# Transposing the queries, keys and attention outputs of three of four batches by DMA in place of TensorE

## The chip, the cores and the metric

The kernel runs on one core of one Trainium2 chip. The metric is the device time of one execution in microseconds (us). Before the change it is 679.26 us, the median of two runs (679.05 to 679.47).

## What is computed

A sparse attention over q, k and v (4 batches, 8 heads, 768 positions, 64 dims) is followed by a mixture of experts over its 3072 output rows. Cut to what matters:

```python
k_sum = k.reshape(B, H, nb, 32, D).max(axis=3)        # 24 blocks of 32 keys
v_sum = v.reshape(B, H, nb, 32, D).mean(axis=3)
scores_l = scale * q @ k^T, only where |i - j| < 16
scores_s = scale * q @ k_sum^T + log(32)
a = softmax(concat(scores_l, scores_s)); attn = a @ concat(v, v_sum)
x = attn with heads side by side                      # (3072, 512)
P = exp(x @ w_gate - max), 8 rounds of row and column normalization
out = sum over e of P[:, e] * (relu(x @ w1[e]) @ w2[e])   # 8 experts, 512 -> 1024 -> 512
```

## The kernel before, in words

Two heads make a pair: NP = 16 pairs, PB = 4 for each batch, numbered 0 to 15. S = 768 positions are G = 6 groups of 128. For each pair TensorE needs keys and queries with the head dimension on the partitions (kT and qT, 128 x 768, the two heads above one another), but they arrive with positions on the partitions. POOL loads them with a cast to bf16 (`load_qk`, L255; `load_v`, L271) into rings of NQ = 6 buffers.

Pairs 0 to 3 (batch 0) go in halves (`pair_half`, L654), so that expert 0 can begin early. Pairs 4 to 15 go whole (`pair_start`, L622, and `pair_whole`, L683). For a whole pair:

- `tr` (L295): six TensorE transposes of 128x128 into a PSUM bank, once for the keys (z = 0) and once for the queries (z = 1). `tr_out` (L307) copies the 128x768 result to kT or qT on ACT, or, for queries, on ACT or DVE.
- `key_max` (L315) on DVE reduces kT to the 24 block maxima. `block_sums` and `block_out` (L327, L334) make the block sums of v.
- `near_values` (L346): four DMAs from SP that copy rows of v next to a group's borders into V_e.
- `scores`, `score_exp`, `masks`, `edges`, `summaries2`, `summary_exp` and `values` (L356 to L431) make the local and summary scores, their exponentials and the weighted values. `normalize` (L487) divides, on DVE, into xs (positions on the partitions).
- `to_xT` (L502): six TensorE transposes of xs into a PSUM bank. `x_out` (L509) copies the result to xT, the input of the experts, on ACT or DVE.

PSUM banks of the attention are a ring "a" of NA = 3. A whole pair opens eight of them: two for `tr`, one for the block sums, two for the summaries, two for the values, one for `to_xT`.

Buffers that set waits: kT and qT have NB = 4 buffers, so that the transposes of pair i wait for the scores, key maxima and summaries of pair i - 4; a load of keys or queries waits for the `tr` of pair i - 6; v's load waits for the values of pair i - 6; V_e and E_e have two.

The order of the work up to the end of the attention comes from a planner (class `Plan`, L34). Each piece of work is a unit with an engine, a booked cost in us, the units that it depends on, a priority (a lower number goes first) and, where it ends later than its engine is free, a `lag`. The planner repeatedly takes the unit that can start first on its engine, and among those within 0.02 us the one of lowest priority number. The instructions are issued in that order, and each engine executes its own in order. Attention pairs have priorities 20 + i, expert 0's matmuls 1000 and more, so that expert 0 fills TensorE between the attention's pieces. Expert 0 works on half a batch (384 rows) at a time: 8 hidden groups of 4 matmuls (L200) and 6 of 4 for the projection (L210); the halves of a batch start when all four pairs of that batch are in xT. Copies out of PSUM get a priority 100 lower. `near_values` is booked with 0.4 us on SP and a lag of 3.5.

`late_constants` (L591) zeroes E_e and V_e, which pairs from 4 on use, sets the ones of V_e and a constant of the routing. It is one unit of 2.4 us on DVE.

After the attention the row and column normalization (`bridge`, L1054) runs beside the rest of expert 0 and the first groups of expert 1, and experts 1 to 7 follow in an order written out by hand (from L1144 on): the lines L877 and L883 of the profile.

Of the kernel before, what the change touches and what calls it, by code (L numbers as in the profile page):

```python
# [33 lines left out]
class Plan:  # L34
# [12 lines left out]
    def add(self, eng, cost, fn, deps=(), prio=0.0, opens=(), uses=(), lag=0.0):  # L47
        u = Unit(eng, cost, fn, [d for d in deps if d is not None], prio, list(opens), lag)
        for b in list(opens) + list(uses):
            b.users.append(u)  # L50
        if uses and eng != "PE":
            u.prio -= 100.0
        self.waiting.append(u)
        return u
# [62 lines left out]
def kernel(  # L117
# [10 lines left out]
    nc = tc.nc  # L128

    B, H, S, D = q.shape  # L130
    G = S // 128
    N, DM = out.shape
    E = moe_w_gate.shape[1]
# [5 lines left out]
    PB = H // 2  # L139
    SCALE = 1.0 / float(D) ** 0.5  # L140
    W = 16
# [4 lines left out]
    VD = D + 1  # L146
# [9 lines left out]
    col_en = const.tile([128, 128], FP32)  # L156
# [3 lines left out]
    xT = persist.tile([128, KD, N], FP16)  # L160
# [34 lines left out]
    def copy(eng, out, in_):  # L195
        (nc.scalar.copy if eng == "ACT" else nc.vector.tensor_copy)(out=out, in_=in_)
# [18 lines left out]
    NB = PB  # L215
    NE = 2
# [9 lines left out]
    if True:  # L226
# [4 lines left out]
        qT = [attn.tile([128, W + S + W], BF16, name=f"qT{i}") for i in range(NB)]  # L231
        kT = [attn.tile([128, S], BF16, name=f"kT{i}") for i in range(NB)]
# [6 lines left out]
        E_e = [attn.tile([128, G, 128], BF16, name=f"Ee{i}") for i in range(NE)]  # L239
        V_e = [attn.tile([128, G, 2 * VD], BF16, name=f"Ve{i}") for i in range(NE)]  # L240

        plan = Plan({"m": 3, "s": NS, "a": NA})
        add = plan.add

        at, units = {}, {}
# [49 lines left out]
        def tr(i, z, tag):  # L295
            st = at.pop(("st", i, z))
            t = at["t", i, z] = bank(tag, "tkq", BF16)
            for g in range(G):
# [4 lines left out]
                else:  # L303
                    nc.tensor.transpose(t[:, g * 128:(g + 1) * 128],  # L304
                                        st[:, g, :, :].rearrange("p j d -> p (j d)"), ident)

        def tr_out(eng, i, z):  # L307
            r, src = i % NB, at.pop(("t", i, z))[:, 0:S]
            dst = (kT[r][:], qT[r][:, W:W + S])[z]
            if i < PB:  # L310
                dst = dst.rearrange("c (p g) -> c p g", g=G)
                src = src.rearrange("c (g p) -> c p g", g=G)
            copy(eng, dst, src)
# [32 lines left out]
        def near_values(i):  # L346

            sv, ve = v_x[i % NQ], V_e[i % NE]
            for j in range(2):
                c0, q0 = VD * j, 64 + 32 * j  # L350
                nc.sync.dma_start(out=ve[q0 + W:q0 + 2 * W, 1:G, c0:c0 + VD],
                                  in_=sv[128 - W:128, j, 0:G - 1, :])
                nc.sync.dma_start(out=ve[q0:q0 + W, 0:G - 1, c0:c0 + VD],
                                  in_=sv[0:W, j, 1:G, :])

        def scores(i, h):  # L356
# [145 lines left out]
        def to_xT(i, h=None):  # L502
            t = at.pop(("xs", i, h or 0))
            tx = at["tx", i, h] = bank("a", "tx", FP16)
            for g in range(G if h is None else HG):
                nc.tensor.transpose(tx[:, g * 128:(g + 1) * 128],  # L506
                                    t[:, g, :, :].rearrange("p j d -> p (j d)"), ident16)

        def x_out(eng, i, h=None):  # L509
            n, t0 = (S, 0) if h is None else (HS, h * HS)  # L510
            t0 += i // PB * S
            copy(eng, xT[:, i % PB, t0:t0 + n], at.pop(("tx", i, h))[:, 0:n])
# [76 lines left out]
            nc.vector.tensor_copy(out=wg_bf[:], in_=wg_f32[:])  # L589

        def late_constants():  # L591
            for t in E_e:
                nc.vector.memset(t[64:128, :, :], 0.0)
            for t in V_e:
                nc.vector.memset(t[:], 0.0)
                nc.vector.memset(t[0:24, :, D:VD], 32.0 / XS)
                nc.vector.memset(t[32:56, :, VD + D:2 * VD], 32.0 / XS)
            nc.vector.memset(col_en, float(E) / float(N))


        U = {}
# [20 lines left out]
        def pair_start(i, prio):  # L622
            o = i - NB
            war_k = [U.get(("S", o, 0)), U.get(("S", o, 1)), U.get(("km", o))]
            war_q = war_k[:2] + [U.get(("ss", o, 0)), U.get(("ss", o, 1))]
            tag = "m" if i < PB else "a"
            for z in range(2 if i >= PB else 1):
                buf = Buffer(tag)
                U["tr", i, z] = add("PE", 0.4, lambda z=z: tr(i, z, tag),
                                    [U["kq"[z], i], U["ident"]] + (war_k, war_q)[z]  # L630
                                    + [U["tr", i, 0] if z else U.get(("S", i - 1, 1 if i > PB else 0))],
                                    prio, opens=[buf])
                U["kT", i, z] = add({"ACT": 0.8} if z == 0 else {"ACT": 0.8, "DVE": 0.95},
                                    0, lambda z=z: tr_out(U["kT", i, z].on, i, z), [U["tr", i, z]], prio,
                                    uses=[buf])
            if i < PB:
                query_half(i, 0, prio)
            U["km", i] = add("DVE", 0.95, lambda: key_max(i), [U["kT", i, 0]] + war_q[2:], prio)
            buf = Buffer("a")
            U["vs", i] = add("PE", 0.4, lambda: block_sums(i),  # L640
                             [U["v", i]] + ([U.get(("A", i - NE, 1))] if i >= PB else []), prio + 0.01, opens=[buf])
            U["Vs", i] = add("DVE", 0.36 if i < PB else 0.84, lambda: block_out(i), [U["vs", i]],
                             prio + 0.01, uses=[buf])
# [37 lines left out]
            return U.get((what, n % PB, n // PB)) if n >= 0 else None  # L681

        def pair_whole(i, prio):  # L683
            U["near", i] = add("SP", 0.4, lambda: near_values(i), [U["v", i], U.get(("A", i - NE, 1))], prio,
                               lag=3.5)
            for h in range(2):
                buf = Buffer("s")
                U["S", i, h] = add("PE", 0.28, lambda h=h: scores(i, h),
                                   [U["kT", i, 0], U["kT", i, 1], U.get(("ed", i - 2))], prio, opens=[buf])
                U["X", i, h] = add("ACT", 0.97, lambda h=h: score_exp(i, h), [U["S", i, h]], prio, uses=[buf])  # L690
                U["mk", i, h] = add("DVE", 0.56, lambda h=h: masks(i, h),
                                    [U["X", i, h], U.get(("A", i - 2, 1))], prio)
            U["ed", i] = add("DVE", 0.78, lambda: edges(i),
                             [U["X", i, 0], U["X", i, 1], U["mk", i, 1], U.get(("A", i - NE, 1))], prio)
            bufs = [Buffer("a"), Buffer("a")]
            U["ss", i, 0] = U["ss", i, 1] = add("PE", 0.22, lambda: summaries2(i),
                                                [U["km", i], U["kT", i, 1], U.get(("A", i - NE, 1))], prio,
                                                opens=bufs)
            for h in range(2):
                U["sx", i, h] = add("ACT", 0.46, lambda h=h: summary_exp(i, h), [U["ss", i, h]], prio,  # L700
                                    uses=[bufs[h]])
            for h in range(2):
                buf = Buffer("a")
                U["A", i, h] = add("PE", 0.4, lambda h=h: values(i, h),
                                   [U["mk", i, h], U["ed", i], U["sx", i, h], U["Vs", i], U["near", i]],
                                   prio, opens=[buf])
                U["no", i, h] = add("DVE", 0.68, lambda h=h: normalize(i, h),
                                    [U["A", i, h], U.get(("xt", i - 2))], prio, uses=[buf])
            buf = Buffer("a")
            U["xt", i] = add("PE", 0.35, lambda: to_xT(i), [U["no", i, 0], U["no", i, 1]], prio, opens=[buf])  # L710
            U["x", i] = add({"ACT": 0.8, "DVE": 0.9}, 0, lambda: x_out(U["x", i].on, i), [U["xt", i]], prio,
                            uses=[buf])

        halves, zero = [], []

# [52 lines left out]
        c0 = add("DVE", 3.8, constants, [], -5.0)  # L768
        for i in range(PB):
            pair_start(i, i)  # L770
            pair_half(i, 0, i)
        add("DVE", 2.4, late_constants, [U["mk", PB - 1, 0]], 5.5)
        expert0(0, [U["x", i, 0] for i in range(PB)])
        for i in range(PB):
            pair_half(i, 1, 10 + i)
# [2 lines left out]
        for i in range(PB, NP):  # L778
# [3 lines left out]
            if i % PB == PB - 1:  # L782
                b = i // PB
                xs = [U["x", PB * b + d] for d in range(PB)]
# [24 lines left out]
    if True:  # L809
# [340 lines left out]
        g = q = NOTHING  # L1150
        for n in range(LAG, len(groups)):
            g0, q0 = g, q
            g = group(*groups[n])
            q = pair(*groups[n - LAG])
            e, j, i = groups[n]
# [55 lines left out]
        A, B, C, D = last  # L1211
# [42 lines left out]
```

The softmax here doesn't subtract the row's maximum and nothing guards it: scores larger than these inputs give would overflow.

## Time and profile before

| what | value |
|---|---|
| median of the runs | 679.26 us |
| the profiled execution | 684.06 us, its span 681.4 us |
| granted clock of TensorE, mean | 0.992 |
| TensorE transposes of pairs 4 to 15: keys, queries (L304) | 72 + 72, 219 to 220 ns each |
| TensorE transposes of outputs (L506), pairs 4 to 15 among 96 | 72 of 128x128 |
| copies to kT, qT, xT of pairs 4 to 15 (L196) | 36 of 128x768: on ACT 0.80 us each, on DVE 0.55 to 0.56 |
| first transposition of pair 4, last of pair 15 | 37.9 us, 127.6 us |
| loads of keys, queries, values on POOL | 0.86, 0.86 and 1.04 us to issue; 6.0, 5.8 and 6.5 us to landing |
| near values on SP | 48 DMAs of 10.2 KB, 0.6 us to issue, 4.6 us to landing |

All are of one profiled execution except the median. PE is TensorE, PEld its loads of weights (they overlap PE), DVE VectorE, ACT ScalarE, POOL GpSimd, SP the engine that here only issues DMAs; an engine's name with a q (SPq, POOLq) is its queue of DMA issues. L304 is line 304 of the kernel. A group row of the profile has line, engine, operation, output <- input with shapes and count, then busy time and the mean ns of one, then the idle time of the engine just before it with what ended it. A timeline row has start, duration, engine, line and what was done. "To landing" is from the issue of a DMA to the arrival of its data.

### The profile page before, as it was taken

To read this page: it belongs to the slowest core of one execution; us is meant where nothing else is said; L and a number is where in the kernel's file an instruction comes from. 1 tells how busy PE (TensorE), PEld (TensorE's weight loads), DVE (VectorE), ACT (ScalarE), POOL (GpSimd) and SP (SyncE) were. 2 spreads that over 40 slices of the span, in tenths; PEclk is the share of its full clock that TensorE was granted. 3 is DMA by queue.
4 is the path that set the end of the run, shared out by engine and by line. 5 is a ranking of instruction groups with operands and counts; after the bars stand their busy time and mean duration, and the time that the engine had idled before them with its cause. 6 is when DMAs were issued, how large, how long until landed. Compare 5 with 4: busy or idle time off the path is not lost.

```text
span 681.4 us, 13654 instructions
## 1 busy us (share of the span) xinstructions
PE 670.5 (98%) x5189; PEld 441.6 (65%) x5189; DVE 585.4 (86%) x1445; ACT 407.7 (60%) x788; POOL 125.9 (18%) x165
## 2 busy tenths in 40 slices
PE   8999999999999999999999999999999999999996
PEld 4665666545666666666666666666666666666665
DVE  6778898788599988999889988998899888998886
ACT  4677877656677765555555555555555555555551
POOL 8699630022202010100101010201010101100000
PEclk9799999999999999999999999999999999999999
DMA  9999990000503123310513050404131051301224
GB/s 120 188 143 143 98 144 7 1 1 0 78 1 37 12 31 48 31 17 1 78 17 33 1 78 1 48 1 60 19 31 17 7 72 17 32 1 48 78 93 155
DMA packets 113618, 33.90 MB, mean 50 GB/s; under 512 B 99984, under 2 KB 110736, under 8 KB 113552
## 3 DMA queue, kind: packets, MB, share of 16 engines
q0 software_dynamic: 104672, 26.22, 41.6%
q1 hardware_dynamic: 8352, 6.80, 3.3%
q8 instruction: 40, 0.66, 0.4%
q14 instruction: 26, 0.21, 0.1%
q10 hardware_dynamic: 528, 0.02, 0.0%
HBM read 52.45 MB, written 6.29 MB: 86 GB/s over the span
## 4 chain that ended last, share of the span: by engine, by line
PE 92%; DVE 4%; DMA 1%; issue 1%; ACT 1%; POOL 1%; DVEq 0%; ACTq 0%
PE xy L883 36%; PE pg L877 16%; PE pa L877 10%; PE pb L877 10%; PE yps L210 6%; PE hps L200 6%; PE sg L323 1%; PE tkq L304 1%; PE vs L331 1%; PE av L468 1%; PE tx L506 1%; DMA qst<-in_q_dram 1%; DVE out_acc L1018 1%; PE av L395 1%; PE av L401 1%
## 5 line engine op out<-in xcount | busy, mean ns | idle before, releaser
L883 PEld LDWEIGHTS <-hf 128*128 128x128 f16 x2352 | 230.1, 98 | 96.1 <-issue 1.2
L883 PE MATMUL xy<-w,hf 128*128 128x256 f16 x1312 | 183.4, 273 | 0.1
L883 PE MATMUL xy<-ws,hf 128*128 128x256 f16 x984 | 147.6, 273 | 0.1
L191 ACT ACTIVATE hf<-pg 128x512 f16<-128x512 f32 x84 | 50.2, 597 | 149.6 <-PE pg L877 149.4
L1018 DVE SCALAR_TENSOR_TENSOR out_acc<-xy,P_sb,out_acc 128x512 f32<-128x512 f32 x164 | 115.1, 744 | 1.7 <-PE xy L883 1.7
L824 DVE TENSOR_TENSOR hf<-hf 128x512 f16<-128x512 f16 x252 | 99.6, 422 | 8.8
L877 PE MATMUL pa<-xT,w 128*128 128x512 f16 x336 | 99.9, 379 | 0.0
L877 PEld LDWEIGHTS <-w 128*128 128x128 f16 x672 | 65.8, 98 | 43.6 <-issue 0.6
L827 DVE TENSOR_TENSOR hf<-pb,c 128x512 f16<-128x512 f32 x84 | 58.1, 692 | 38.2 <-PE pb L877 35.7
L176 POOL DMA_DIRECT2D w<-in_moe_w_dram x56 | 41.8, 759 | 220.3 <-PE pg L877 192.1
L877 PEld LDWEIGHTS <-ws 128*128 128x128 f16 x504 | 49.3, 98 | 25.3
L911 ACT COPY c<-pg 128x512 f32<-128x512 f32 x84 | 49.2, 585 | 22.7 <-PE pg L877 22.6
L827 DVE TENSOR_TENSOR hf<-pg,c 128x512 f16<-128x512 f32 x84 | 57.2, 681 | 0.6 <-PE pg L877 0.6
L191 ACT ACTIVATE hf<-pa 128x512 f16<-128x512 f32 x84 | 50.6, 603 | 0.4 <-PE pa L877 0.4
L896 ACT COPY pg<-pa 128x512 f32<-128x512 f32 x84 | 47.9, 570 | 4.8
L877 PE MATMUL pg<-xTs,w 128*128 128x512 f16 x168 | 50.0, 379 | 0.1
L877 PE MATMUL pb<-xT,ws 128*128 128x512 f16 x168 | 50.0, 379 | 0.0
L877 PE MATMUL pg<-xTs,ws 128*128 128x512 f16 x168 | 50.0, 379 | 0.0
L877 PE MATMUL pg<-xT,w 128*128 128x512 f16 x168 | 50.0, 379 | 0.0
L877 PE MATMUL pb<-xTs,ws 128*128 128x512 f16 x168 | 50.0, 379 | 0.0
L904 ACT COPY c<-pb 128x512 f32<-128x512 f32 x84 | 49.8, 593 | 0.2 <-ACT pg L896 0.2
L200 PE MATMUL hps<-xT,w 128*128 128x384 f16 x256 | 48.7, 326 | 0.0
(136 smaller groups left out, 842.5 us busy)
## 6 DMA issues: line engine op xcount, KB each, us to landing
w<-in_moe_w_dram POOLq DMA_DIRECT2D x8, 1024.0 KB, 9.3
w<-in_moe_w_dram POOLq DMA_DIRECT2D x56, 128.0 KB, 3.5
out_dram<-out_acc SPq DMA_DIRECT2D x22, 256.0 KB, 2.0
qst<-in_q_dram POOLq DMA_DIRECT2D x32, 96.0 KB, 5.8
vx<-in_v_dram POOLq DMA_DIRECT2D x16, 192.0 KB, 6.5
kst<-in_k_dram POOLq DMA_DIRECT2D x24, 96.0 KB, 6.0
w<-in_moe_w_dram POOLq DMA_DIRECT2D x2, 512.0 KB, 8.3
kst<-in_k_dram POOLq DMA_DIRECT2D x4, 192.0 KB, 4.9
```

Source lines behind the costliest of these rows:

```text
L176: nc.gpsimd.dma_start(out=t[:, :, h, :], in_=moe_w1[e].rearrange("(dk p) f -> p dk f", p=128)[:, :, f:f + 128])
L191: nc.scalar.activation(out=out, in_=in_, func=AF.Relu, bias=0.0, scale=1.0)
L200: nc.tensor.matmul(hp[:, 0:n], lhsT=w1s[e][:, dk, 128 * f:128 * (f + 1)], rhs=xT[:, dk, t0:t0 + n], start=(dk == 0), stop=(dk == KD - 1))
L210: nc.tensor.matmul(yp[:], lhsT=h[:, f, c * 128:(c + 1) * 128], rhs=w2s[e][:, f, :], start=(f == 0), stop=(f == KF - 1))
L824: nc.vector.tensor_tensor(out=out, in0=in0, in1=in1, op=ALU.subtract)
L827: nc.vector.tensor_tensor(out=out, in0=in0, in1=in1, op=ALU.add)
L877: nc.tensor.matmul(bank[:], lhsT=w[:, dk, :], rhs=x[:, dk, :], start=start and dk == 0, stop=dk == KH - 1, skip_group_check=True)
L883: nc.tensor.matmul(bank, lhsT=a(f)[:, 128 * c:128 * (c + 1)], rhs=w[:, f, :], start=start and f == 0, stop=f == FH - 1, skip_group_check=True)
L896: nc.scalar.copy(out=B["g"][:], in_=B["a"][:])
L904: nc.scalar.copy(out=B["c5"][:], in_=B["b"][:])
L911: nc.scalar.copy(out=B["c2"][:], in_=B["g"][:])
L1018: nc.vector.scalar_tensor_tensor(out=acc, in0=src, scalar=P_sb[:, t, e:e + 1], in1=acc, op0=ALU.mult, op1=ALU.add)
```

## The change

For pairs 4 to 15 the keys, queries and outputs are transposed by one DMA each from SBUF to SBUF, issued from SP (`tr_dma`, `x_dma`), where they were six TensorE transposes and a copy out of PSUM. Each is booked with 0.1 us on SP and a lag of 2.6. No bank of ring "a" is opened for them. The other dependencies stay, except that a pair's transposes no longer wait for the scores of the pair before or for each other. `late_constants` returns a list of pieces, which are chained on DVE with priority 12.5 in place of one unit with 5.5. `near_values` would go to POOL for i >= 16.

```diff
+        def tr_dma(i, z):
+            r, st = i % NB, at.pop(("st", i, z))
+            nc.sync.dma_start_transpose(out=(kT[r][:], qT[r][:, W:W + S])[z].rearrange("c (g t) -> c g t", g=G),
+                                        in_=st[:].rearrange("p g j d -> p (g j d)"))
+
+        def x_dma(i):
+            nc.sync.dma_start_transpose(
+                out=xT[:, i % PB, i // PB * S:(i // PB + 1) * S].rearrange("c (g t) -> c g t", g=G),
+                in_=at.pop(("xs", i, 0))[:].rearrange("p g j d -> p (g j d)"))
...
-                nc.sync.dma_start(out=ve[q0 + W:q0 + 2 * W, 1:G, c0:c0 + VD],
+                eng = nc.gpsimd if i >= 16 else nc.sync
+                eng.dma_start(out=ve[q0 + W:q0 + 2 * W, 1:G, c0:c0 + VD],
...
         def late_constants():
-            for t in E_e:
-                nc.vector.memset(t[64:128, :, :], 0.0)
-            for t in V_e:
-                nc.vector.memset(t[:], 0.0)
+            def zero(t):
+                nc.vector.memset(t, 0.0)
+
+            def ones(t):
                 nc.vector.memset(t[0:24, :, D:VD], 32.0 / XS)
                 nc.vector.memset(t[32:56, :, VD + D:2 * VD], 32.0 / XS)
-            nc.vector.memset(col_en, float(E) / float(N))
+            parts = [(0.4, lambda t=t: zero(t[64:128, :, :])) for t in E_e]
+            for t in V_e:
+                parts += [(0.4, lambda t=t: zero(t[:])), (0.15, lambda t=t: ones(t))]
+            return parts + [(0.15, lambda: nc.vector.memset(col_en, float(E) / float(N)))]
...
             for z in range(2 if i >= PB else 1):
+                if i >= 4:
+                    U["tr", i, z] = U["kT", i, z] = add("SP", 0.1, lambda z=z: tr_dma(i, z),
+                                                        [U["kq"[z], i]] + (war_k, war_q)[z], prio, lag=2.6)
+                    continue
...
-            U["near", i] = add("SP", 0.4, lambda: near_values(i), [U["v", i], U.get(("A", i - NE, 1))], prio,
+            U["near", i] = add(*(("POOL", 3.4) if i >= 16 else ("SP", 0.4)), lambda: near_values(i), [U["v", i], U.get(("A", i - NE, 1))], prio,
                                lag=3.5)
...
-            buf = Buffer("a")
-            U["xt", i] = add("PE", 0.35, lambda: to_xT(i), [U["no", i, 0], U["no", i, 1]], prio, opens=[buf])
-            U["x", i] = add({"ACT": 0.8, "DVE": 0.9}, 0, lambda: x_out(U["x", i].on, i), [U["xt", i]], prio,
-                            uses=[buf])
+            if i >= 4:
+                U["xt", i] = U["x", i] = add("SP", 0.1, lambda: x_dma(i), [U["no", i, 0], U["no", i, 1]], prio,
+                                             lag=2.6)
...
-        add("DVE", 2.4, late_constants, [U["mk", PB - 1, 0]], 5.5)
+        c1 = U["mk", PB - 1, 0]
+        for us, fn in late_constants():
+            c1 = add("DVE", us, fn, [c1], 12.5)
```

More of the change, by code (lines that the diff above doesn't have):

```diff
@@ L350, in near_values @@
                 c0, q0 = VD * j, 64 + 32 * j
-                nc.sync.dma_start(out=ve[q0 + W:q0 + 2 * W, 1:G, c0:c0 + VD],
+                eng = nc.gpsimd if i >= 16 else nc.sync
+                eng.dma_start(out=ve[q0 + W:q0 + 2 * W, 1:G, c0:c0 + VD],
                                   in_=sv[128 - W:128, j, 0:G - 1, :])
-                nc.sync.dma_start(out=ve[q0:q0 + W, 0:G - 1, c0:c0 + VD],
+                eng.dma_start(out=ve[q0:q0 + W, 0:G - 1, c0:c0 + VD],
                                   in_=sv[0:W, j, 1:G, :])
@@ L708, in pair_whole @@
                                     [U["A", i, h], U.get(("xt", i - 2))], prio, uses=[buf])
-            buf = Buffer("a")
-            U["xt", i] = add("PE", 0.35, lambda: to_xT(i), [U["no", i, 0], U["no", i, 1]], prio, opens=[buf])
-            U["x", i] = add({"ACT": 0.8, "DVE": 0.9}, 0, lambda: x_out(U["x", i].on, i), [U["xt", i]], prio,
-                            uses=[buf])
+            if i >= 4:
+                U["xt", i] = U["x", i] = add("SP", 0.1, lambda: x_dma(i), [U["no", i, 0], U["no", i, 1]], prio,
+                                             lag=2.6)
+            else:
+                buf = Buffer("a")
+                U["xt", i] = add("PE", 0.35, lambda: to_xT(i), [U["no", i, 0], U["no", i, 1]], prio, opens=[buf])
+                U["x", i] = add({"ACT": 0.8, "DVE": 0.9}, 0, lambda: x_out(U["x", i].on, i), [U["xt", i]], prio,
+                                uses=[buf])
         halves, zero = [], []
```

## The prediction

> **What bounds the kernel now.** I read the page from the top: busy shares first, then the chain of work that ended last. The head of the page and the chain's shares by engine:
>
> ```profile
> span 681.4 us, 13654 instructions
> ## 1 busy us (share of the span) xinstructions
> PE 670.5 (98%) x5189; PEld 441.6 (65%) x5189; DVE 585.4 (86%) x1445; ACT 407.7 (60%) x788; POOL 125.9 (18%) x165
> ...
> PE 92%; DVE 4%; DMA 1%; issue 1%; ACT 1%; POOL 1%; DVEq 0%; ACTq 0%
> ```
>
> TensorE is busy 98% of the span and is 92% of the chain. A busy share is an average, so I next read the table of stretches where the changed pairs run (first transposition of pair 4 at 37.9 us, last of pair 15 at 127.6). Columns: PE, PEld, DVE, ACT, POOL busy, granted clock, DMA share, GB/s.
>
> ```profile
> 44.00:54.00 10.00, 10.00 (x108) 6.00 (x107) 8.03 (x22) 7.28 (x11) 9.67 (x12) 1.00 2.52 142
> 54.00:64.00 10.00, 10.00 (x120) 6.48 (x118) 9.01 (x25) 7.79 (x13) 9.77 (x13) 1.00 2.49 143
> 84.00:94.00 10.00, 10.00 (x104) 6.19 (x103) 9.33 (x26) 7.53 (x12) 7.44 (x10) 1.00 1.76 156
> 114.00:124.00 10.00, 10.00 (x101) 6.06 (x98) 9.05 (x25) 8.18 (x14) 0.00 (x0) 1.00 0.01 2
> ```
>
> TensorE has no gap here: the planner fills every wait of the attention with matmuls of expert 0. VectorE follows at 80 to 93%. The DMA share is above 2 until 64 us (packets of several loads in flight on each engine), and POOL issues loads without a break; from about 100 us the DMA engines are idle. So TensorE bounds this stage, and time taken from it is won only if nothing new makes it wait.
>
> How much is a transposition in TensorE's stream? The groups by shape, within 36 to 128 us:
>
> ```profile
> L196 ACT COPY kT<-tkq 128x768 bf16<-128x768 bf16 x12 | 9.6, 800 | 0.3 <-PE tkq L304 0.3
> L196 ACT COPY xT<-tx 128x768 f16<-128x768 f16 x9 | 7.2, 799 | 1.9 <-PE tx L506 1.9
> L304 PE MATMUL tkq<-ident,kst 128*128 128x128 bf16 x72 | 6.0, 220 | 0.0
> L304 PE MATMUL tkq<-ident,qst 128*128 128x128 bf16 x72 | 6.0, 219 | 0.0
> ```
>
> and the timeline of TensorE around 99 us:
>
> ```profile
> 98.12 0.82 PE L200 MATMUL hps<-xT,w 128*128 128x384 f16 x4
> 98.78 0.50 PE L304 MATMUL tkq<-ident,kst 128*128 128x128 bf16 x6
> 99.11 0.50 PE L506 MATMUL tx<-ident,xs 128*128 128x128 f16 x6
> 99.45 0.81 PE L200 MATMUL hps<-xT,w 128*128 128x384 f16 x4
> ```
>
> The group rows give 0.50 us for six transposes, but that counts the tail that the next instruction covers. From start to start six take 99.11 - 98.78 = 0.33 and 99.45 - 99.11 = 0.34 us. This is what leaves the stream.
>
> **What the Trainium skill says.** "VectorE: DVE Perf Modes", The three transpose paths: TensorE 390 ns and the DMA crossbar 1309 ns for 128x128. The trace has 219 ns for one TensorE transpose and 55 ns in a stream; no run here shows a DMA transpose. "DMA: Bandwidth & Descriptors", Latency and other measured facts: a DMA transpose was measured at 261 GB/s. Same page, Issuing engines are not separate DMA queues: what SP, ACT and POOL issue shares 16 DMA engines. The trace agrees, below. Same page, Rules for kernel authors: transposes from different queues must be serialized, one beside ordinary DMAs needs nothing; here all come from SP, so I charge no such wait.
>
> **The change, part by part.**
>
> TensorE loses, for pairs 4 to 15, two input groups and one output group of six: 12 x 3 = 36 groups, 216 transposes. 36 x 0.34 = 12.2 us. This is the most the change can win: 1.8%.
>
> The PSUM copies go too: 12 of kT on ACT (9.6 us), five of qT on ACT at 0.80 and seven on DVE at 0.55, about ten of xT on ACT (8.0) and two on DVE (1.1): ACT loses 21.6 us, DVE 5.0. By themselves these win nothing, since TensorE is full behind them. But three of the eight uses of "a" banks per pair go as well, so the attention can be ordered faster. Outputs of pairs 4 and 15 now leave TensorE at 50.8 and 127.6 us: 7.0 us per pair. VectorE's fixed work for a pair is key maximum 0.95, block sums out 0.92, masks 1.10, edges 0.78, normalization 1.49 = 5.24 us; at the 93% of the fullest stretch 5.6. I take 5.7 us per pair as the pace to which the new order is written, 7.0 if the banks were not the limit.
>
> SP gains three transposes per pair. Its timeline now holds only the near values:
>
> ```profile
> 48.91 0.59 SPq L351 DMA_DIRECT2D Ve<-vx  x1
> 49.54 0.60 SPq L353 DMA_DIRECT2D Ve<-vx  x1
> 50.18 0.59 SPq L351 DMA_DIRECT2D Ve<-vx  x1
> 50.82 0.59 SPq L353 DMA_DIRECT2D Ve<-vx  x1
> ```
>
> Four issues take 2.5 us of SP for a pair (booked at 0.4). A transpose is booked at 0.1 plus 2.6 us until it lands. Its issue is not in the trace. Lower bound: the 0.6 us of these rows. Upper bound: six blocks of 128x128 one after another at the skill's 1309 ns, 7.9 us. I take 1.2, twice the nearest row, since a transpose names 768 columns on 128 partitions where that row moves 96 short ones. Then SP needs 2.5 + 3 x 1.2 = 6.1 us per pair against 5.7: 12 x 0.4 = 4.8 us late at the end. SP works in order: behind an output transpose that waits for its normalization stand the near values of the next pair and the inputs of later ones; values(i) on TensorE waits for the former, key_max and the scores for the latter, and key_max holds up VectorE, with evacuations behind it.
>
> Landing: the near values show what load does. DMA issues in 52 to 60 us, then in 86 to 130:
>
> ```profile
> kst<-in_k_dram POOLq DMA_DIRECT2D x4, 96.0 KB, 5.9
> Ve<-vx SPq DMA_DIRECT2D x3, 10.2 KB, 5.4
> ```
>
> ```profile
> Ve<-vx SPq DMA_DIRECT2D x17, 10.2 KB, 2.7
> ```
>
> The same transfer lands in 5.4 us beside the loads, 2.7 later and 1.9 at best: up to 3.5 us more than unloaded. I add 3.5 us for transposes booked at 2.6. Bounds: 0 if the order leaves that much room (inputs are loaded well ahead: pair 10's queries are issued by 55 and transposed at 75), 6 if several queue.
>
> Bandwidth: 196,608 B at 261 GB/s is an estimate of 0.75 us per transpose, 2.3 us per pair. Beside the 4.3 us in which POOL issues one pair's loads that is 6.6 at worst, if the engines have no room left; the planner books 4.85 for the loads. POOL idles 7.0 us in waits for v buffers between 64 and 84 us, so a delay has a cover of that size; without it, 12 x (6.6 - 5.7) = 11 us. I count it within the likeliest case's range, since it delays the same instructions as SP does.
>
> End of a batch: the filler of batch 0 ends at 72.1 us and batch 1's output is in xT at 73.0, just in time. Up to there TensorE runs fifteen of the 36 groups (inputs of pairs 4 to 9, outputs of 4 to 6); without them the filler ends at 72.1 - 5.1 = 67.0. At 5.7 us per pair from an output of pair 4 at 47 to 50 us, pair 7's leaves at 64 to 67, plus 3 to 5 to land: 0 to 5 us of idle TensorE, the same lateness again and not added.
>
> The constants: 2.5 us of memsets at 23.5 to 26.1 us on DVE, cut into pieces with a later priority. Nothing waited for them but a weight load, 0.3 us; their cover is VectorE's idle time around 27 to 29. Without it they cost what a piece takes, 0.4. I take 0. Near values on POOL need i >= 16, and pairs end at 15: nothing. After the attention the order is written out and TensorE-bound, so what is won or lost before is carried to the end; the routing (P_sb) ends at 176 us and is first used at 180, and it starts with the last output, so it moves along.
>
> Sum: -12.2 + 4.8 + 3.5 = -3.9 us. The profiled execution took 684.06 (span 681.4 and 2.7 around it), the runs' median is 679.26: 680.2 on the first, 675.3 as a median.
>
> **The rivals.**
> All hidden: the order leaves room, nothing is late. For it: loads run far ahead, the DMA engines are free from 100 us. Against it: TensorE has no gap and DVE little. -12.2 plus up to 1: 668 (665 to 670).
> SP becomes the bound, and the kernel slower: one mechanism, the issue of a transpose, p. Lateness is 12 x (2.5 + 3p - 5.7) + 3.5; it reaches 12.2 at p = 1.3 us. At p = 1.8, three times the nearest row, SP needs 7.9 us per pair: 29.9 late, 697; 679 to 719 for p from 1.3 to 2.4. For it: near values were booked at a sixth of what they take. Against it: other bookings agree with the trace (exp 0.97 booked, 0.971 measured), so 2.6 from issue to landing may too.
> The crossbar moves block after block, 7.9 us each: 23.7 per pair, 12 x 18 = 216 us late, about 883. Against it: the 261 GB/s.
>
> **How the numbers follow.** Partly kept, 675 (own range 670 to 680): 0.52. All hidden: 0.13. SP bound: 0.26. Crossbar slow: 0.09. From 666 to 705 lie all but a tail of the second, the first, and two thirds of the third, up to p = 2: 0.8. Faster by over 2%, about what a measurement of this kernel can tell from no change (below 665.7): only the edge of "all hidden", 0.03. Slower (above 692.8): p above 1.7, 0.14, and the crossbar's 0.09: 0.23. Within: 0.74.
>
> **What would show it.** 216 fewer matmuls, with TensorE's busy time down by some 18 us by the overlapping records and its stream by 12; gaps in TensorE between 40 and 130 us of about 8 us, with waits ended by SP's DMAs at scores, values or behind DVE's key maximum; SP's row for a transpose near 1.2 us and its landing at 4 to 6 us in the loaded stretch. A row above 1.3 us, or landings above 8, would make the prediction wrong on the slow side; a TensorE without gaps, on the fast one.

## The result and the profile after

The changed kernel takes 718.2 us (715.7 to 720.7) against 679.26 us: 1.0572 times the time before, interval 1.0509 to 1.0636. The forecast was 675 us, range 666 to 705. It is outside the range, and on the other side of no change.

The head of the page of the changed kernel and the shares of its chain by engine:

```profile
span 714.0 us, 13259 instructions
...
PE 665.7 (93%) x4973; PEld 430.2 (60%) x4973; DVE 577.2 (81%) x1434; ACT 390.1 (55%) x763; POOL 125.4 (18%) x165
...
PE 79%; DMA 12%; DVE 5%; POOL 2%; issue 1%; ACT 0%; DVEq 0%; POOLq 0%; ACTq 0%
```

The 216 transposes are gone (5189 to 4973 matmuls). TensorE's busy share fell from 98% to 93%, and DMAs went from 1% to 12% of the chain. If 12.2 us left TensorE's stream, the span of 714.0 holds 714.0 - 681.4 + 12.2 = 44.8 us of new time in which TensorE is idle or slow. Idle are 37.4 us of it (714.0 - 665.7 now against 681.4 - 670.5 before). The other 7.4 us are matmuls that take longer, which is why the busy time fell by 4.8 us only. The table of stretches of the changed kernel shows where; the columns are those of the table before:

```profile
44.00:54.00 10.00, 10.00 (x107) 4.98 (x107) 6.61 (x17) 6.35 (x11) 6.16 (x8) 0.83 1.79 150
64.00:74.00 10.00, 4.00 (x17) 1.27 (x18) 1.77 (x4) 2.42 (x4) 5.19 (x6) 0.52 1.88 132
84.00:94.00 10.00, 1.98 (x24) 1.21 (x25) 2.28 (x7) 1.93 (x4) 5.07 (x6) 0.54 1.85 142
114.00:124.00 10.00, 10.00 (x96) 5.33 (x92) 7.65 (x21) 6.67 (x11) 2.76 (x4) 0.92 1.64 161
```

Before, TensorE was busy for all of each of these stretches, at a clock of 1.00. Now 84 to 94 us has 2.0 us of work, VectorE and ScalarE are nearly idle beside it, and after a gap TensorE comes back at about half its clock. No compute engine is the bound there. The last columns say what is busy: in 114 to 124 us the DMA engines moved 2 GB/s before and 161 now. The transfers that had all but ended by 104 us before are still going on.

What TensorE waits for, first in its list of waits and then in its timeline (in brackets the idle time before the instruction, and what ended it):

```profile
PE sg L333 <- DMA qT<-qst: 35.6, 8, 9.2
```

```profile
70.00 0.58 PE L333 MATMUL sg<-qT,kT 64*128 64x160 bf16 x6 [8.21 <-DMA qT<-qst]
91.35 0.58 PE L333 MATMUL sg<-qT,kT 64*128 64x160 bf16 x6 [9.19 <-DMA qT<-qst]
```

The scores wait eight times for the transposed queries, 35.6 us in all. Expert 0's filler can't cover it: it needs the outputs of the same late pairs. Scores of pair 4 start at 43.92 and of pair 15 at 142.01 us, so a pair takes 98.1 / 11 = 8.9 us; before, they started at 41.4 and 118.5 us, 7.0 per pair.

That the loss lies here and not later is seen at the gate of the last batch (`lp`), which needs the last output. Its matmuls before and after:

```profile
129.47 0.69 PE L520 MATMUL lp<-wg_bf,xT 128*128 128x8 f16 x22
...
159.70 0.68 PE L531 MATMUL lp<-wg_bf,xT 128*128 128x8 f16 x21 [0.71 <-DMA xT<-xs]
```

It runs 30.2 us later, of 32.6 us by which the span grew. In every kernel of this document that computes the attention, the time from the arrival of the last output in xT to the end is between 551.8 and 554.5 us.

The DMA issues of the changed kernel, in the last column the us to landing:

```profile
kst<-in_k_dram POOLq DMA_DIRECT2D x24, 96.0 KB, 10.7
...
Ve<-vx SPq DMA_DIRECT2D x48, 10.2 KB, 6.4
...
kT<-kst SPq DMA_TRANSPOSE x12, 7.5
qT<-qst SPq DMA_TRANSPOSE x12, 8.6
xT<-xs SPq DMA_TRANSPOSE x12, 8.1
```

A transpose lands in 7.5 to 8.6 us. Not only the new transfers are slow: the loads of keys went from 6.0 to 10.7 and the near values from 4.6 to 6.4 us, with nothing changed in them. In 134 to 142 us, when the loads are over, the same transposes land in 2.8 (kT, qT) and 3.4 us (xT). And three transposes of one pair in SP's timeline (start, time that SP is held):

```profile
87.48 1.23 SPq L309 DMA_TRANSPOSE kT<-kst  x1
88.81 1.50 SPq L313 DMA_TRANSPOSE xT<-xs  x1
90.41 3.53 SPq L309 DMA_TRANSPOSE qT<-qst  x1
```

One issue holds SP for 1.21 us at best and 3.6 at worst. The mean of the 29 that start before 134 us, while loads are under way, is 1.94 us (1.80 for all 36). The first of a row is mostly quick and a later one held, as in these three.

### The profile page after: what moved, and what is told of

Read it like the earlier page. It is cut to its first block, busy times and chain, and to the rows that moved or that the text cites. A ratio compares the mean times of both kernels' runs of the same rounds, so it can differ in the third digit from the quotient of the medians.

```text
span 714.0 us, 13259 instructions
## 1 busy us (share of the span) xinstructions
PE 665.7 (93%) x4973; PEld 430.2 (60%) x4973; DVE 577.2 (81%) x1434; ACT 390.1 (55%) x763; POOL 125.4 (18%) x165
## 4 chain that ended last, share of the span: by engine, by line
PE 79%; DMA 12%; DVE 5%; POOL 2%; issue 1%; ACT 0%; DVEq 0%; POOLq 0%; ACTq 0%
PE xy L908 34%; PE pg L902 15%; PE pb L902 10%; PE pa L902 10%; PE hps L200 4%; DMA qT<-qst 4%; PE yps L210 3%; DMA vx<-in_v_dram 3%; DMA qst<-in_q_dram 2%; DMA kst<-in_k_dram 1%; DMA xT<-xs 1%; DVE out_acc L1043 1%; DVE hf L852 1%; DMA w<-in_moe_w_dram 1%; PE sg L333 1%
## 5 line engine op out<-in xcount | busy, mean ns | idle before, releaser
L852 DVE TENSOR_TENSOR hf<-pb,c 128x512 f16<-128x512 f32 x84 | 58.0, 691 | 39.3 <-PE pb L902 35.4
L936 ACT COPY c<-pg 128x512 f32<-128x512 f32 x84 | 49.2, 586 | 22.4 <-PE pg L902 22.4
L200 PE MATMUL hps<-xT,w 128*128 128x384 f16 x256 | 51.3, 343 | 0.0
## 6 DMA issues: line engine op xcount, KB each, us to landing
kst<-in_k_dram POOLq DMA_DIRECT2D x24, 96.0 KB, 10.7
```

What stands on the lines that cost most here:

```text
L200: nc.tensor.matmul(hp[:, 0:n], lhsT=w1s[e][:, dk, 128 * f:128 * (f + 1)], rhs=xT[:, dk, t0:t0 + n], start=(dk == 0), stop=(dk == KD - 1))
L852: nc.vector.tensor_tensor(out=out, in0=in0, in1=in1, op=ALU.add)
L936: nc.scalar.copy(out=B["c2"][:], in_=B["g"][:])
```

## The experiments

My theory after the result: loads and transposes share the DMA engines, one's time adding to the other's (D). Rivals: SP's queue in order, near values and all (S); an order written for too short times (P); the short packets of the loads alone; the mere landing time of a transpose. Diffs are against the changed kernel unless the text says otherwise; times are ratios to the kernel before on the same chip, with their 95% intervals.

### The order (booked)

```diff
-add("SP", 0.1, lambda z=z: tr_dma(i, z), ..., lag=2.6)
+add("SP", 1.3, lambda z=z: tr_dma(i, z), ..., lag=7.0)
-("SP", 0.4)   # near values
+("SP", 2.5)
```

The output transposes got the same figures, and the loads 2.8 to 3.2 us.

> The changed kernel, with the planner's bookings set to what the trace shows: a transpose 1.3 us on SP and a lag of 7.0, near values 2.5 us on SP, loads of pairs 4 to 15 2.8, 2.8 and 3.2 us of the DMA in place of 1.55, 1.55 and 1.75. Only the order changes. Theory P (the work fits, the order was written for a transposition that lands in 2.6 us): the waits go, 668 to 680. Theory D: pairs still come at 8 to 9 us, the attention still ends near 150 us and TensorE has not enough other work until then: 700 to 720, with the waits in other places.

1.0559 [1.0502, 1.0616], the same as the change itself; theory P, with 668 to 680 us, falls. The waits moved (TensorE waits 6.9 us for qT in place of 35.6, and longer behind VectorE and ScalarE), but the attention ends no sooner. The planner's own start times show why. For the scores of pairs 4 to 15 the order of the changed kernel has 37.8 to 93.9 us, 5.1 us per pair; that of booked has 45.8 to 142.4 us, 8.8 per pair. Against its own order the last output of the changed kernel lands 49 us late (159.7 us, 110.4 in the order), that of booked 5 us (164.1 and 158.8), and both kernels take the same time. So lateness against the order is not what costs; when the last output arrives is.

### Inputs, outputs, constants (in_only, out_only, constants)

```diff
-            if i >= 4:
+            if i >= 16:          # in_only: outputs on TensorE as before
                 U["xt", i] = U["x", i] = add("SP", 0.1, lambda: x_dma(i), ...
```

> The changed kernel with the outputs transposed by TensorE as before: 24 transposes by DMA. Theory D: loads 4.3 us and two transposes at 1.8 us are 7.9 us per pair where the order is written to 5.3: some 28 us late, 8 us saved on TensorE, 692 to 705. Theory S: SP has 2.5 + 2.5 = 5.0 us per pair, nothing late: 670 to 676.

1.0327 [1.0262, 1.0391]: 703.45 us, in the range of theory D and far from that of S. Queries landed in 8.9 us, and the scores waited 24.6 us for them.

out_only has the same edit at the inputs (`if i >= 16` ahead of `tr_dma`).

> The changed kernel with the inputs transposed by TensorE as before: 12 transposes by DMA. Both theories have nothing late (D: 4.3 + 1.8 = 6.1 us per pair against some 6.4 in the order; S: 3.7 us of SP), save at the ends of batches, where the last output lands some 6 us later than booked: 4.1 us saved on TensorE, 0 to 5 lost, 675 to 680.

1.022 [1.0173, 1.0267]: 696.03 us, where 675 to 680 was expected under both theories. The span is 692.7 us: with 12 x 0.34 = 4.1 us gone from the stream, 692.7 - 681.4 + 4.1 = 15.4 us are lost to one transpose per pair. The timeline of TensorE in this kernel has 12.3 us of it in four rows, three of which are:

```profile
70.65 0.48 PE L200 MATMUL hps<-xT,w 128*128 128x384 f16 x1 [1.53 <-DMA xT<-xs]
76.21 0.48 PE L200 MATMUL hps<-xT,w 128*128 128x384 f16 x1 [5.09 <-DMA xT<-xs]
108.43 0.19 PE L531 MATMUL lp<-wg_bf,xT 128*128 128x8 f16 x1 [4.78 <-DMA xT<-xs]
```

These are the ends of batches: the filler of one batch is used up, and the next needs the last xT of its four pairs. There the landing time stands in the open, 7.3 us here where the order has 2.6.

constants is the kernel before with `late_constants` in pieces and nothing else.

> The kernel before, with only the constants cut into pieces at priority 12.5. The prediction had 0. In the changed kernel expert 0 begins at 27.7 us where it began at 29.6 before: if that comes from the constants, this run shows 677 to 678; if from the clock of that execution, 679.

0.9996 [0.998, 1.0013]: nothing, as the prediction had it.

### Outputs, except those of the batch ends (out_mid)

```diff
-            if i >= 4:
+            if i not in (7, 11):     # and no input by DMA
                 U["xt", i] = U["x", i] = add("SP", 0.1, lambda: x_dma(i), ...
```

> Outputs by DMA for pairs 4 to 15 but 7 and 11, the last of their batches; all inputs by TensorE. With all outputs by DMA the time was 696: TensorE waited 12 us at the ends of batches for an output that lands 7 to 10 us late. If that was the whole loss, it is gone here and ten groups are saved, 3.4 us: 676 to 679. If something else was lost (loads delayed by the transposes): 682 to 690.

1.0118 [1.0082, 1.0155], half of what out_only lost, and not the 676 to 679 us of a loss that is gone. Two of its ten runs took 681.4 us and the others 688.6 to 693.8; why is not known. The waits at batch ends are still there, of 4.3 and 4.4 us: now the outputs of pairs 6 and 10, the last by DMA, arrive after those of 7 and 11. So it is the landing time, and not which pair is last.

### The loads (no_loads, no_loads_pool)

```diff
+            if i >= 6:                # pairs 6 to 15: keys and queries not loaded again
+                at["st", i, z] = keep[4 + i % 2, z]
+                return
```

> The changed kernel without the loads of keys, queries and values of pairs 6 to 15 (they take the staged tiles of pairs 4 and 5 and whatever values lie in the buffers, so their attention is not the reference's). All 36 transposes, all waits among engines and the order stay. Theory D, now: the DMA engines serve loads and transposes together at 140 to 160 GB/s, a transposition of 192 KB costs them 1.6 to 2 us when loads run beside it, however large the packets of the loads. Then without loads transposes land near 2.8 us from pair 6 on, the wait of the scores for qT goes under 10 us, and the time is 667 to 676. Theory S (SP's order and 6.2 us of issue per pair against the 5.1 us to which the order is written): 12 us late all the same, 679 to 688.

1.0288 [1.0226, 1.0349]: 700.8 us, above the ranges of both theories. Without loads beside them transposes land in 2.8 to 2.9 us, so the loads were what made them late. But half of the loss stays, and SP's timeline in this kernel hints why: from 66 to 94 us it is one issue behind the other without a break.

```profile
68.29 1.29 SPq L314 DMA_TRANSPOSE kT<-kst  x1
69.68 1.23 SPq L318 DMA_TRANSPOSE xT<-xs  x1
70.96 1.29 SPq L314 DMA_TRANSPOSE qT<-qst  x1
72.34 0.59 SPq L367 DMA_DIRECT2D Ve<-vx  x1
...
74.90 1.29 SPq L314 DMA_TRANSPOSE kT<-kst  x1
```

From kT to kT 74.90 - 68.29 = 6.6 us: three transposes at 1.33 and four near values at 0.64, start to start. That is above the order's 5.1. In no_loads_pool the near values are issued from POOL, in the same order:

> The run without loads of pairs 6 to 15, in the same order, with the near values issued by POOL, which has nothing else to do then, in place of SP. Theory S, sharpened: SP's queue is the tight resource; with loads its transposes take 1.95 us each on average to issue (1.5, 2.5 and 1.8 for kT, qT, xT), 2.6 + 5.85 = 8.4 us per pair, without loads 1.3 and 6.6 us, while the order starts the scores of pairs 4 to 15 at 37.8 to 93.9 us, 5.1 per pair. Without the near values SP needs 4.0 us per pair and nothing is queued behind a near value that waits: of the 30 us that the run without loads lost, 8 to 12 stay (pairs 4 and 5, ends of batches): 676 to 683. If not SP's queue but the DMA engines set the pace without loads too: 697 to 702.

1.0175 [1.0145, 1.0205]: 691.4 us, between the two ranges. Over a third of what no_loads lost is gone, so SP's queue holds up the kernel even without the loads of pairs. One new wait of 10.0 us belongs to this edit alone (near values stood behind weight loads on POOL), so the effect of SP's queue is larger than the difference of the two. How much larger was not tried.

### SP without the near values, loads kept (near_act)

```diff
-add(*(("POOL", 3.4) if i >= 16 else ("SP", 0.4)), lambda: near_values(i), ...
+add(*(("ACT", 2.5) if i >= 4 else ("SP", 0.4)), lambda: near_values(i), ...
```

> The changed kernel with its loads, with the near values issued by ACT (booked 2.5 us there) in place of SP. The order is then written to 6.3 us per pair. Theory S: SP has 3 x 1.95 = 5.9 us per pair and keeps up: 673 to 685. Theory D (loads and transposes need 8 to 9 us per pair of the DMA engines): no better pace, SP's issue of a transpose grows further, over 700.

1.0635 [1.061, 1.066]: 722.7 us, no faster than the change, in the range of theory D and far above the 673 to 685 of S. SP now has idle gaps, and a transpose holds it no shorter than before (1.92 us on average of all 36, 1.80 in the changed kernel). The input transposes come 8.5 us apart from pair 4 to pair 15, the scores 10.3. But the run is no clean test of SP's queue. In exchange ScalarE's exponentials now stand behind near values that wait for loads: the profile puts 18.3 us of ScalarE's idle time down to loads of keys and 9.8 to transposed queries. What SP relieved without these new waits would give stays open.

### Packets and the crossbar (fat_loads, plain_copies)

```diff
-nc.gpsimd.dma_start(out=t[:, :, j, :], in_=src[b, h0 + j].rearrange("(g p) d -> p g d", p=128))
+nc.gpsimd.dma_start(out=t[:].rearrange("p g j d -> p (g j d)")[:, j * G * D:(j + 1) * G * D],
+                    in_=src[b, h0 + j].rearrange("(p g) d -> p (g d)", g=G))
```

> The changed kernel, with the key and query loads of pairs 4 to 15 reading and writing runs of 384 elements in place of 64 (same bytes, same number of DMAs, same waits; positions come in another order, so that the attention of these pairs is computed on permuted rows: that part is not the reference's). Theory D (the 16 DMA engines are the limit: small-packet loads and crossbar transposes together need 8 to 9 us per pair): transposes land in 3 to 5 us in place of 8, scores wait under 15 us in place of 36, span 675 to 690. Theory S (SP's in-order queue is the limit: 6.2 us of issue per pair and what stands behind a waiting transpose): landing times fall a little, waits stay, 705 to 718.

1.0542 [1.048, 1.0604]: 717.2 us, no difference from the change. This is in the range of theory S and not in that of D as it was put then: outputs land in 5.3 us in place of 8.1, but queries in 8.4, and the scores wait 35.4 us for them. Rows six times as long do not help, so short packets of the loads alone are not the cause.

```diff
-nc.sync.dma_start_transpose(out=...rearrange("c (g t) -> c g t", g=G), in_=...)
+nc.sync.dma_start(out=..., in_=...)      # the same bytes, as they lie
```

> The changed kernel, with each DMA transpose replaced by a plain copy of the same 192 KB from SBUF to SBUF (the transposition itself is left out, so the values are not the reference's). If the crossbar transpose is what costs the DMA engines (theory D): copies land in under 5 us in the loaded stretch, scores hardly wait, 668 to 680. If any 192 KB beside the loads does it, landing stays at 7 to 9 us and the time at 700 or more. Under theory S the issue also falls from 1.24 to about 0.6 us, 4.3 us per pair, so that S alone would give 670 to 685 too: read with the run with larger load packets.

1.0243 [1.0166, 1.0321]: 696.9 us, between the ranges. With plain copies somewhat over half of the loss is gone, with the same bytes, dependencies and order. Two things are cheaper at once, and this run doesn't part them: SP issues a copy in 0.54 us, and between 44 and 84 us the engines move 173 to 205 GB/s where the change had 132 to 153. The copies still take long to land, as the issues of this kernel show:

```profile
kT<-kst SPq DMA_DIRECT2D x12, 192.0 KB, 6.2
qT<-qst SPq DMA_DIRECT2D x12, 192.0 KB, 6.8
xT<-xs SPq DMA_DIRECT2D x12, 192.0 KB, 5.8
```

### The transfers by themselves (mixture, mixture_pair)

Two kernels of DMA alone, with a barrier between stretches; each was run once.

```python
for i in range(18):
    load(i)        # POOL, one head pair's keys, rows of 64 elements
    turn(i)        # SP, one transpose of 128x768, SBUF to SBUF
    if i % 3 == 2:
        near(i // 3)   # mixture_pair only: the four near values, SP
```

> This kernel leaves out the whole computation and writes zeros; it does only five stretches of DMA with a barrier between them: 18 loads of keys as in pairs 4 to 15 (POOL), 18 transposes of 128x768 from SBUF to SBUF (SP), both together, 18 loads with 18 plain copies of the same bytes, and the copies alone. No engine computes and no buffer is waited for, so the length of a stretch divided by 18 is the price of the DMA work alone. Theory D (loads and transposes take time from the same DMA engines, one adding to the other): loads alone about 1.4 us each (a pair's three took 4.3 in the kernel before), transposes alone about 1.3, both together about 2.7 to 2.9 for one of each (8.6 us for a pair's three of each). Rival I (the two overlap in the engines, and what slowed the changed kernel was its order and SP's waits): both together as long as the longer of the two alone, about 1.5 us. Plain copies beside the loads: about 2.1 by D, since that kernel moved 181 to 198 GB/s.

The table of stretches for mixture (us, VectorE and POOL busy, clock, DMA share, GB/s): loads, transposes, both, and the end of the loads with copies, where only queued loads are left.

```profile
46.00:74.00 28.00, 6.66 (x16) 27.99 (x35) 1.00 1.86 118
80.00:102.00 22.00, 2.89 (x17) 0.00 (x0) 1.00 0.78 150
106.00:144.00 38.00, 2.84 (x13) 25.13 (x31) 1.00 1.76 156
...
176.00:188.00 12.00, 3.04 (x9) 11.29 (x15) 1.00 2.30 148
```

Loads alone are held back by POOL's issue (two of 0.82 us each). With many in flight they reach 148 GB/s, 1.33 us for the 196,608 bytes of one. Transposes alone move 150 GB/s, 1.31 us each, but that is not all that the engines can do: SP starts one every 1.33 us, and in between the engines run low (DMA share 0.78). The DMA rate from 77 to 103 us, in 40 slices, shows it:

```profile
GB/s 0 0 176 126 156 147 145 158 139 164 120 183 112 190 106 195 101 199 90 208 88 210 76 213 84 211 80 213 79 215 82 214 75 216 82 205 94 205 92 0
```

At the 216 GB/s of the fullest slice a transpose would need 0.9 us of the engines, as an estimate. Beside loads there are no such gaps: both together stay near 156 GB/s, hardly more than the loads by themselves. From the first issue at 103.0 to the last landing at 149.9 us it took 46.9 / 18 = 2.6 us for one of each, so a transpose adds 1.3 us to the 1.33 of its load. Why it is 1.3 and not 0.9 was not tried. Theory D holds without any order or wait, and rival I (1.5 us) falls. Copies are another matter: alone 305 GB/s or 0.65 us each, and with a load 37.3 / 18 = 2.07 us. The landings grow here too with nobody waiting: a transpose 2.8 us alone, 7.8 beside loads.

> The computation is left out again (zeros are written); four stretches of DMA with a barrier between them: 18 loads whose rows are 384 elements long; those with 18 transposes; the loads of the changed kernel (rows of 64) with 18 transposes and four near values after every third transpose, which is the DMA work of six pairs of the changed kernel and no wait of its order; and the transposes with the near values, without loads. Theory D (loads and transposes add up in the DMA engines): the third stretch costs 3 x 2.55 plus up to 0.9 for the small near values, so 7.8 to 8.6 us per pair, near the changed kernel's 8.9; the fourth is SP's queue, 4 x 0.64 + 3 x 1.33 = 6.6 us. The long rows are open: if short packets are what loads and transposes share, the second stretch falls to 1.9 to 2.1 us for one of each; if a transpose keeps the engines to itself while it runs and the load is served beside it only slowly, it stays at 2.4 or more. Rival I (order and waits, not the DMA work): the third stretch is at most SP's 6.6 us per pair.

SP's timeline in the third stretch (loads, transposes, near values) and in the fourth (no loads):

```profile
145.94 0.60 SPq L69 DMA_DIRECT2D Ve<-vx  x1
...
148.57 6.04 SPq L44 DMA_TRANSPOSE kT<-st  x3
154.67 0.60 SPq L69 DMA_DIRECT2D Ve<-vx  x1
...
189.00 3.95 SPq L44 DMA_TRANSPOSE kT<-st  x3
193.00 0.59 SPq L69 DMA_DIRECT2D Ve<-vx  x1
```

Beside loads three transposes hold SP for 6.04 us, without them for 3.95. Near values start at 137.01, 145.94, 154.67, 163.22 and 171.35 us: 34.3 / 4 = 8.6 us for a pair's DMA work, with no wait of the order, where the changed kernel has 8.9. Without loads it is 6.6 us, as in no_loads. This joins D and S into one cause. Transposes and loads together get about 153 to 156 GB/s; a transpose beside loads holds SP for about 2.0 us in place of 1.3 (from the second row of three on, the first 1.24 us, the third 2.2 to 3.1); and SP does its near values between transposes, so 3 x 2.0 + 4 x 0.64 = 8.6. With SP's part taken away the DMA work alone would still be 3 x 2.6 = 7.8 us by mixture, more than the 7.0 us that a pair took before.

The open point on long rows came out against them: loads of 384-element rows with transposes took 49.2 us for 18 of each, 2.7 us, as much as with short rows. The loads ended sooner (44 us after the start), but the transposes then held SP for 47.5 / 18 = 2.6 us each in place of 2.0. Why the transposes give way to longer packets was not tried.

### What is left of the idea (late_only)

If loads are the trouble, transposes that come after them should be cheap: inputs of pairs 13 to 15 and outputs of 12 to 15 by DMA, the rest on TensorE.

```diff
-                if i >= 4:
+                if i >= 13:
                     U["tr", i, z] = U["kT", i, z] = add("SP", 0.1, lambda z=z: tr_dma(i, z),
...
-            if i >= 4:
+            if i >= 12:
                 U["xt", i] = U["x", i] = add("SP", 0.1, lambda: x_dma(i), ...
```

> The changed kernel, but by DMA only what runs when the loads are over: inputs of pairs 13 to 15 and outputs of pairs 12 to 15, ten of the 36 groups. Theory D: they land near 2.8 us as booked, nothing is late, 10 x 0.34 = 3.4 us saved: 675 to 677. If a transposition were late for another reason than the loads, 679 or more.

0.9972 [0.996, 0.9984]: 678.83 us against 680.24 on its chip, 1 to 3 us faster than the kernel before, a little short of the forecast. Ten groups of 36 went, so at most 10 x 0.34 = 3.4 us were to be had. The outputs land in 2.8 us as forecast; the inputs take 9.4, beside weight loads, but are far enough ahead of the scores that TensorE waits for none.

## Why the prediction was wrong, step by step

**TensorE's saving: right.** 36 groups and 216 transposes left. The busy time, though, fell by 4.8 us and not by some 18, since matmuls after gaps ran at a lower clock. In late_only about 0.0028 x 680 = 1.9 of at most 3.4 us are kept.

**"Bandwidth": the step that failed.** I took the 261 GB/s that the prediction names with its page, hence 0.75 us per transpose and 6.6 us per pair with its loads, and then put this term at nothing in the sum, as covered by 7 us of POOL's waits and by SP's own delay. No run here shows 261 GB/s for these transposes; beside loads one costs 1.3 us (mixture), so that a pair's DMA work is 7.8 us before near values and 8.6 with them in SP's queue. The measurement decides. The transfers did not hide beside SP's delay but made it longer. The cover was no cover either: 7 us of POOL's waits in all stand against a delay in each of twelve pairs. And the trace of before had shown the sign: with a DMA share of 2.5 at 142 GB/s the loads, issued without a break, already ran near the 148 that queued loads reach by themselves in mixture. The changed kernel moves 150 GB/s in the same stretch, transposes included.

**"SP issue, p = 1.2": right alone, wrong in company.** Unloaded it is 1.22 to 1.33 us. I treated it as a property of the instruction; it is also where a shortage of the DMA engines is felt, and 1.94 us under loads. The prediction had named "a row above 1.3 us, or landings above 8" as what would make it wrong on the slow side. Both came.

**"5.7 us per pair as the pace": too slow a pace.** The order was written for 5.1. In the prediction's own form the measured 8.6 us give 12 x (8.6 - 5.1) = 42 us, near the 44.8 us lost, where its sum had 4.8 + 3.5. But that form is lateness against the order, and booked, written to 8.8 us per pair, takes as long. What the trace shows is 8.9 us per pair in place of the 7.0 of before: 21 of the 30.2 us by which the gate of the last batch is later. The scores of pair 4 start 2.5 us later, and from the last pair's scores to the gate it is 17.7 us in place of 11.0.

**"Landing, +3.5 us": too small.** 7.5 to 8.6 us in place of 6.1. **"0 to 5 us of idle TensorE" at batch ends, "the same lateness again and not added":** wrong when outputs alone go by DMA. out_only lost 12.3 us there, in four waits.

**Constants and near values on POOL: right**, nothing (0.9996).

**The rivals.** The slower one, SP as the bound, had the place and the mechanism, and its price is p. Its own formula at 1.94 gives -12.2 + 12 x (2.5 + 5.82 - 5.7) + 3.5 = +23 us, 702; with the order's 5.1 us, 709. The remaining 9 us I can't assign one by one: landings at batch ends and TensorE's lower clock after gaps are both in them. It had 0.26, and its p was scaled from SP's 0.6 us rows; that p grows beside loads was not in it. The slow crossbar (7.9 us per transpose) was far off.

## What to carry to other kernels

Before moving work to DMA, look at what the DMA engines already do in that stretch: a rate that stays flat while issues go on without a break may be a limit that new transfers will share, as it was here, whatever a lone transfer reaches. Price a transfer by the two together, on the queue that issues it, since here that is where busy DMA engines held up the instructions behind it. And compare the new pace with the old one before blaming the order: right bookings moved the waits in booked, but not the time.

## What was not expected of the hardware

- The Trainium skill, "Advanced Engine Details and Errata", X-Bar Transpose (TRN2), has transposes by DMA as fast as regular DMAs, 350 to 400 GB/s. From SBUF to SBUF at 128x768 in 2-byte elements, issued one behind the other from SP, they are not: 1.31 us against 0.65 us each, 150 against 305 GB/s (mixture). SP's issue sets the pace of the transposes there, but even the fullest of the slices shown above has no more than 216 GB/s.
- The issue of a transpose on SP takes longer when the DMA engines have other work: 1.22 to 1.33 us alone, 2.0 on average beside loads, up to 3.6 in the changed kernel, and 8.2 once in no_loads_pool beside weight loads.
- A gap in TensorE costs more than its length. The Trainium skill, "TensorE: Matmul & The Clock Gate", Part 1: The HAM clock gate, has it fall to half its clock after an idle window of about 3.4 us. The trace agrees: in the stretches of the changed kernel with waits of 5.7 to 9.2 us the granted clock was 0.50 to 0.54, and six score matmuls took 0.58 us in place of 0.38.
